# K's transposition on VectorE in 32x32 blocks instead of on TensorE, with K loaded in two halves, in a cached-attention and MLP decode kernel

## The chip, the cores and the metric

One Trainium2 chip, one core, float32 throughout. The metric is the device time of one execution in microseconds.

## The reference

A decode step of one transformer block (8 sequences, one token each) with adaptive layer norm. What is computed:

```python
mod = (silu(c) @ w_mod).reshape(8, 6, 1, 512)      # sa, ca, ga, sb, cb, gb
h = layernorm(x) * (1 + ca) + sa
x = x + ga * attention(h)
h = layernorm(x) * (1 + cb) + sb
x = x + gb * mlp(h)

def attention(x):                  # 32 query heads, 8 key heads, Dh = 128
    W = 2048                       # of 8192 cached keys, the last 2048 are used
    q = (x @ wq)                   # 512 -> 32*128
    k = repeat(k_cache[:, :, -W:], 4); v = repeat(v_cache[:, :, -W:], 4)
    p = softmax(q k^T * Dh**-0.5)
    return (p v) @ wo              # 32*128 -> 512

def mlp(x):                        # F = 1792
    r = max(x @ w1 + b1, 0)
    return (r * r) @ w2 + b2
```

The 8 sequences times 8 key heads give 64 pairs, each with a K and a V of 2048 x 128 numbers (1 MB each).

## The kernel before

**Loads.** All large loads are issued by the sync engine (SP) from one list, in a fixed order, into two "big" buffers (128 partitions x 32 KB: one K tile, which is four sequences of one key head, 4 MB) and five "small" ones (16 KB: one V tile, which is two sequences of one key head, 2 MB, or a piece of w_mod, wq or wo). `loads` (line 143) begins K0, w_mod in four pieces, wq in four pieces, K1, V0, K2, V1, K3, V2, V3, K4, and goes on with a K and two V in turn; biases, the last rows of wo, w1 and w2 end it. `pump` issues as long as the next load of the list has a free buffer. `done(key)` gives a buffer back and calls `pump`; SP then waits until the last reader of that buffer has finished, and every later load stands behind it.

In a K tile, partition 4p + u holds 64 successive keys of sequence u. `k` below is that tile as 64 columns (keys) of 128 numbers.

**The loop** (line 502) runs over the 32 halves of the 16 K tiles plus a lag of `PV_LAG` = 5 steps for V, and is written out by hand: nothing reorders it (`manual_schedule`). Each engine works through its own instructions in this order.

- `transposes(q, g, e)` (lines 223 to 238): eight transpositions of 128x128 by TensorE against the identity into PSUM (`kt_ps`), in two groups of four; ScalarE copies the first group out to `kT`, VectorE the second. Two calls (e = 0, 1) fill one of three `kT` buffers (four sequences of 512 columns). Eight calls make one K tile; the last gives the buffer back.
- `scores(q, g)` (346 to 364): four matmuls, one for each sequence u of the tile, with 32 columns of `qwin` stationary and the 512 columns `kT[:, u]` moving, into quarter u of the PSUM tile `s_ps`, which gathers all scores of one key head (two K tiles). `qwin` is a zero-padded window over q, so that each of the eight calls lands in rows of its own.
- `window(hk)` (343): one VectorE copy from `qall` into `qwin`.
- `soft_a` to `soft_d` (366 to 439): the softmax of one key head: copy out, row maximum, maximum over the rows of a pair (two small matmuls), exponential with its sum, a copy that doubles the columns, eight transpositions by TensorE, and two VectorE multiplications with the mask `mine` into `pT`.
- `weighted(n, h)` (441): P times V, four matmuls a call; after the second call of a V tile VectorE folds the result into `o_sb` with four instructions (464 and 466).
- `gather`, `project_o`: every fourth step, transposition of the head's output and its product with wo.

**The start.** While w_mod arrives, three quarters of K0 are transposed (`EARLY`, line 263, lets the loop skip them; the last quarter comes in the loop's step 0), between the matmuls on w_mod. After the last piece of wq, `turn_q(0)` (328) copies the first half of q out, turns it by four TensorE transpositions and copies it to `qall` (line 334); `turn_q(1)` does the second half in step 1. Then the scores begin.

**The end.** After the last V: output projection, residual, second layer norm, MLP; `spin` puts idle matmuls between.

Of the kernel before, what the change touches and what calls it, by code (L numbers as in the profile page):

```python
# [8 lines left out]
F32 = mybir.dt.float32  # L9
# [11 lines left out]
def tile_adaln_cached_attention_mlp(  # L21
# [15 lines left out]
    P = 128  # L37
# [18 lines left out]
    ktp = ctx.enter_context(tc.tile_pool(name="ktp", bufs=3))  # L56
    ps_kt = ctx.enter_context(tc.tile_pool(name="ps_kt", bufs=2, space=bass.MemoryType.PSUM))
# [32 lines left out]
    def load(key):  # L90
# [7 lines left out]
        if kind in "KV":  # L98
# [6 lines left out]
            v = v[:, SK - W :, :].rearrange("u (p j) d -> p u (j d)", p=P // v.shape[0])  # L105
# [79 lines left out]
    qall = consts.tile([P, HKV, B, REP], F32, name="qall")  # L185
    qwin = [consts.tile([P, B, 60], F32, name=f"qwin{i}") for i in range(2)]
    for t in qwin:
        nc.gpsimd.memset(t, 0.0)

# [8 lines left out]
    u4 = consts.tile([P, 4], F32, name="u4")  # L198
    nc.vector.tensor_reduce(u4, ident.rearrange("p (u x) -> p u x", u=4), axis=AX.X, op=ALU.add)
    for c in range(2):  # L200
        nc.vector.tensor_scalar(bq[:, 4 * c : 4 * c + 4], u4, uq[:, c : c + 1], None, op0=ALU.mult)
# [11 lines left out]

    mine = consts.tile([P, 2, REP], F32, name="mine")
    odd = ident.rearrange("p (r u) -> p u r", u=2)
    for u in range(2):
        nc.vector.tensor_reduce(mine[:, u, 0:1], odd[:, u, :], axis=AX.X, op=ALU.add)
        for t in range(1, REP):
            nc.vector.tensor_copy(mine[:, u, t : t + 1], mine[:, u, 0:1])

    KTS = {}

    def transposes(q, g, e):

        k = slot(("K", q), DH)
        if e == 0:
            KTS[q, g] = ktp.tile([P, 4, 16, 32], F32, name="kT")
        t = KTS[q, g]
        for a in range(2):
            p = ps_kt.tile([P, 4, P], F32, name="kt_ps")  # L230
            for i in range(4):
                nc.tensor.transpose(p[:, i, :], k[:, 32 * e + 16 * a + 4 * g + i, :], ident)  # L232
            i = 8 * e + 4 * a
            (nc.vector.tensor_copy if a else nc.scalar.copy)(  # L234
                t[:, :, i : i + 4, :], p.rearrange("p i (r u) -> p u i r", u=4)
            )
        if g == 3 and e == 1:
            done(("K", q))
# [24 lines left out]
    EARLY = [(0, g) for g in range(4)]  # L263
# [400 lines left out]
```

## Time and profile before

| | |
|---|---|
| median of 3 runs | 396.94 us (396.89 to 397.75) |
| the profiled execution | 397.39 us, of which the span from first to last instruction is 395.6 |
| TensorE busy | 330.5 us (84%) |
| VectorE busy | 178.2 us (45%) |
| ScalarE busy | 97.5 us (25%) |
| q1, the queue with all loads | 164.71 MB, 97.9% of 16 engines' span |
| read from HBM | 164.77 MB |
| mean granted clock of TensorE | 0.974 |

Busy time of an engine is the time in which it ran an instruction; idle time of an engine that is not the bottleneck costs nothing. In rows of groups the columns are line, engine, operation, output and inputs, shapes and count, then busy microseconds and the mean nanoseconds of one, then the idle time ahead of them and what ended it. In rows of stretches: from and to, length, busy time (count) of TensorE's matmuls, of its weight loads, of VectorE, ScalarE and GpSimd, the granted clock, the mean busy share of the 16 transfer engines, and GB/s. In rows of time: start, length, engine, line, operation. "PEld" is a weight load, "SPq" the queue of the engine that issues the loads.

### The profile page before, as it was taken

The numbers are of one execution on the slowest core, as the hardware profiler recorded it, in microseconds if no ns is written. First come the engines' busy times: TensorE is split into PE (matmuls) and PEld (weight loads), VectorE is DVE, ScalarE is ACT, GpSimd is POOL, SyncE is SP. The second block draws the span as 40 slices with busy tenths as digits, with TensorE's granted clock in tenths as the row PEclk, the third lists the DMA queues.
The fourth block names the chain that finished last, engine by engine and source line by source line (L and its number), as shares of the span: only waits on it lengthen the run. The fifth ranks groups of instructions, "written<-read, shape, count | busy, mean of one in ns | idle before, by whom it ended". The sixth has DMA issues, their size and how long they took to land.

```text
span 395.6 us, 5981 instructions
## 1 busy us (share of the span) xinstructions
PE 330.5 (84%) x2550; PEld 162.4 (41%) x2550; DVE 178.2 (45%) x416; ACT 97.5 (25%) x169; POOL 2.4 (1%) x12
## 2 busy tenths in 40 slices
PE   0683489979998697999889988998859998997696
PEld 0440035554454353444444544444534454432133
DVE  6121023454456353655464556454524455455531
ACT  2220022342232122322332222222211241222010
POOL 2000000000000000000000000000000000000000
PEclk9996889999999998999999999999999999999999
DMA  8999999999999999999999999999999999999993
GB/s 335 410 430 427 441 418 442 417 419 446 404 435 442 414 432 422 441 417 451 403 449 409 444 416 434 434 419 421 437 419 447 417 437 413 431 431 421 422 424 136
DMA packets 10363, 165.22 MB, mean 418 GB/s; under 512 B 1112, under 2 KB 1376, under 8 KB 1632
## 3 DMA queue, kind: packets, MB, share of 16 engines
q1 hardware_dynamic: 10192, 164.71, 97.9%
q8 instruction: 20, 0.33, 0.3%
q10 hardware_dynamic: 144, 0.13, 0.1%
q14 instruction: 7, 0.06, 0.0%
HBM read 164.77 MB, written 0.07 MB: 417 GB/s over the span
## 4 chain that ended last, share of the span: by engine, by line
DMA 46%; PE 42%; DVE 7%; ACT 4%; issue 1%; ACTq 0%; DVEq 0%
DMA big<-in_A_k_cache_dram 31%; PE kt_ps L232 20%; PE s_ps L358 9%; PE o_ps L450 7%; DMA small<-in_A_wq_dram 6%; DMA big<-in_B_w_dram 5%; DMA small<-in_A_v_cache_dram 4%; ACT pr L402 2%; DVE o_sb L466 2%; DVE kT L234 2%; PE m_ps L294 1%; ACT kT L234 1%; DVE pT L429 1%; PE m_ps L319 1%; DVE pr L410 1%
## 5 line engine op out<-in xcount | busy, mean ns | idle before, releaser
L232 PE MATMUL kt_ps<-ident,big 128*128 128x128 f32 x1024 | 145.5, 285 | 22.6 <-DMA big<-in_A_k_cache_dram 18.3
L232 PEld LDWEIGHTS kt_ps<-ident,big 128*128 128x128 f32 x1024 | 112.8, 144 | 111.9 <-ACT kT L234 68.1
L234 DVE COPY kT<-kt_ps 128x512 f32<-128x512 f32 x128 | 88.2, 689 | 121.5 <-PE kt_ps L232 121.5
L234 ACT COPY kT<-kt_ps 128x512 f32<-128x512 f32 x128 | 75.0, 586 | 209.4 <-PE kt_ps L232 208.6
L358 PE MATMUL s_ps<-kT,qwin 128*32 128x512 f32 x512 | 69.2, 614 | 0.8 <-DVE qwin L344 0.8
L450 PE MATMUL o_ps<-small,pT 128*32 128x512 f32 x512 | 67.1, 602 | 1.9 <-DMA small<-in_A_v_cache_dram 1.9
L466 DVE SCALAR_TENSOR_TENSOR o_sb<-o_ps,diag,o_sb 128x128 f32<-128x128 f32 x96 | 33.7, 351 | 3.4
L319 PE MATMUL m_ps<-small,h1T 128*32 128x512 f32 x64 | 11.5, 857 | 11.5 <-DMA small<-in_A_wq_dram 11.5
L450 PEld LDWEIGHTS o_ps<-small,pT 128*32 128x32 f32 x512 | 11.7, 108 | 22.7 <-issue 22.7
L464 DVE TENSOR_SCALAR o_sb<-o_ps,diag 128x128 f32<-128x128 f32 x32 | 11.2, 350 | 16.3 <-PE o_ps L450 15.6
L358 PEld LDWEIGHTS s_ps<-kT,qwin 128*32 128x32 f32 x512 | 10.3, 109 | 12.8 <-issue 11.1
L402 ACT ACTIVATE pr<-ss,nm 128x512 f32<-128x512 f32 x8 | 9.9, 1244 | 11.8 <-DVE nm L399 11.7
L334 DVE COPY qall<-m_ps 128x128 f32<-128x128 f32 x2 | 0.8, 390 | 23.0 <-PE m_ps L333 23.0
L435 PE MATMUL m_ps<-zs,tsel 128*128 128x8 f32 x16 | 3.1, 266 | 8.7 <-DVE pT L429 8.7
L319 PEld LDWEIGHTS m_ps<-small,h1T 128*32 128x32 f32 x64 | 2.1, 134 | 19.8 <-DMA small<-in_A_wq_dram 10.6
L429 DVE TENSOR_TENSOR pT<-m_ps,mine 128x512 f32<-128x512 f32 x16 | 10.2, 680 | 0.0
L474 PE MATMUL m_ps<-o_sb,pick 128*128 128x512 f32 x16 | 8.4, 606 | 1.8 <-DVE o_sb L466 1.6
L426 PEld LDWEIGHTS m_ps<-ident,pr 128*128 128x128 f32 x64 | 6.9, 141 | 7.0 <-issue 7.0
L426 PE MATMUL m_ps<-ident,pr 128*128 128x128 f32 x64 | 8.7, 278 | 1.1 <-DVE zs L412 1.1
L370 DVE TENSOR_REDUCE mx<-ss 128x1 f32<-128x512 f32 x8 | 5.5, 688 | 8.6 <-ACT ss L368 8.6
L410 DVE COPY pr<-pr 128x512 f32<-128x512 f32 x8 | 3.4, 430 | 12.3 <-ACT pr L402 12.3
L294 PE MATMUL m_ps<-small,cT 128*32 128x512 f32 (+1 forms) x64 | 6.6, 531 | 1.3 <-DMA small<-in_w_mod_dram 1.3
(123 smaller groups left out, 105.4 us busy)
## 6 DMA issues: line engine op xcount, KB each, us to landing
big<-in_A_k_cache_dram SPq DMA_DIRECT2D x16, 4096.0 KB, 21.9
small<-in_A_v_cache_dram SPq DMA_DIRECT2D x32, 2048.0 KB, 23.2
small<-in_A_wq_dram SPq DMA_DIRECT2D x4, 2048.0 KB, 21.8
small<-in_w_mod_dram SPq DMA_DIRECT2D x4, 1536.0 KB, 17.4
small<-in_A_wo_dram SPq DMA_DIRECT2D x3, 2048.0 KB, 19.9
big<-in_A_wo_dram SPq DMA_DIRECT2D x2, 1024.0 KB, 17.8
big<-in_B_w_dram SPq DMA_DIRECT2D x1, 2048.0 KB, 23.4
big<-in_B_w_dram SPq DMA_DIRECT2D x1, 1792.0 KB, 22.0
```

Of the source, the lines that this page charges most:

```text
L232: nc.tensor.transpose(p[:, i, :], k[:, 32 * e + 16 * a + 4 * g + i, :], ident)
L234: (nc.vector.tensor_copy if a else nc.scalar.copy)(t[:, :, i : i + 4, :], p.rearrange("p i (r u) -> p u i r", u=4))
L294: nc.tensor.matmul(pm[32 * q : 32 * q + 32, : (m1 - m0) * P].rearrange("p (m n) -> p m n", n=P), cT[:, kc, :], wv[:, m0:m1, q, :], start=( ...
L319: nc.tensor.matmul(pqs[r][32 * g : 32 * g + 32, :], hT[:, kc, :], w[:, 4 * r + g, :], start=(kc == 0), stop=(kc == NQ - 1),)
L358: nc.tensor.matmul(s_ps[0][32 * u : 32 * u + 32, :], qwin[hk % 2][:, 4 * c + u, o : o + 32], kT[:, u].rearrange("p i r -> p (i r)"), start ...
L402: nc.scalar.activation(pr.rearrange("p i (r e) u -> p e i r u", e=2)[:, :, :, :, 0], SS_.pop(hk).rearrange("p (e i r) -> p e i r", e=2, i= ...
L426: nc.tensor.transpose(pp[:, i * P : (i + 1) * P], pr[:, 4 * a + i].rearrange("p r u -> p (r u)"), ident)
L429: nc.vector.tensor_mul(PT_[hk][:, a].rearrange("p x i r -> p i x r"), pp.rearrange("p (i x r) -> p i x r", i=4, r=2 * REP), mine.rearrange ...
L450: nc.tensor.matmul(o[32 * g : 32 * g + 32].rearrange("p j d -> p (j d)"), PT_[hk][:, h, 4 * c + g].rearrange("p i r -> p (i r)"), v[:, j : ...
L464: nc.vector.tensor_scalar(d, o[:, 0, :], diag[:, 0:1], None, op0=ALU.mult)
L466: nc.vector.scalar_tensor_tensor(d, o[:, j, :], diag[:, j : j + 1], d, op0=ALU.mult, op1=ALU.add)
L474: nc.tensor.matmul(pp, pick.rearrange("p t u -> p (t u)"), o.rearrange("p c d -> p (c d)"), start=True, stop=True)
```

## The change

K's transposition goes to VectorE, whose transposition turns each 32x32 block of its operand in place. `transposes(q, j, e)` is now one VectorE instruction: 32 keys of each partition times the 32 numbers from 32j on, 1024 columns, written to `kT` in order. Eight calls still make a tile, but what lies on `kT`'s partitions is now 32 of the 128 numbers, for each of four groups of 32 partitions. So q is laid out in blocks: `turn_q` copies q with four instructions of 32 partitions each to `qbd`, and `window` multiplies it by `sel` on TensorE and copies the product with eight instructions (four each of ScalarE and VectorE) to `qst`. `scores` keeps four matmuls of 512 columns a call, but reads from `kT` pairs of columns, two out of every eight. For that the keys are spread otherwise over the partitions: each K is loaded by two DMAs, x = 0 and 1, into every second partition.

The rows of the scores then stand in another order. `soft_b` has one more matmul (128x512, with the permutation `perm`), the exponential reads its result from PSUM; the masked doubling is one instruction each of VectorE and ScalarE, and `soft_d` turns P with one VectorE transposition of 128x1024 instead of eight of TensorE and two multiplications. `kT` has two buffers instead of three, of the same size; the PSUM pool `ps_kt` is gone. `EARLY` holds half of K0, and the other half comes in the loop's step 1.

On SP each K is now two issues. Before, from the last piece of wq on (`big` a K buffer, `small` a V buffer):

```order
L113 DMA small_95<-in_A_wq_dram 128x4096
L108 DMA big_92<-in_A_k_cache_dram 128x1x8192
L108 DMA small_96<-in_A_v_cache_dram 128x1x4096
L108 DMA big_91<-in_A_k_cache_dram 128x1x8192
L108 DMA small_97<-in_A_v_cache_dram 128x1x4096
L108 DMA big_92<-in_A_k_cache_dram 128x1x8192
```

And now, at the same place:

```order
L117 DMA small_92<-in_A_wq_dram 128x4096
L107 DMA big_89<-in_A_k_cache_dram 64x1x8192 x2
L112 DMA small_93<-in_A_v_cache_dram 128x1x4096
L107 DMA big_88<-in_A_k_cache_dram 64x1x8192 x2
L112 DMA small_94<-in_A_v_cache_dram 128x1x4096
L107 DMA big_89<-in_A_k_cache_dram 64x1x8192 x2
```

The list is the same, each K stands in it twice with 64 partitions.

On VectorE, from the two halves of q (L334, `qall`) to the second K tile, before (L234 are the copies of K's transpositions out of PSUM, L344 the window):

```order
L310 TENSOR_SCALAR mul<-m_ps,lo 128x128
L334 COPY qall<-m_ps 128x4x32
L344 COPY qwin_115<-qall 128x8x4
L234 COPY kT<-kt_ps 128x4x128 x2
L334 COPY qall<-m_ps 128x4x32
L234 COPY kT<-kt_ps 128x4x128 x3
L344 COPY qwin_116<-qall 128x8x4
L234 COPY kT<-kt_ps 128x4x128 x6
L370 TENSOR_REDUCE mx<-ss 128x1
```

And now (L330 are the copies of q, L348 those of the window, L230 K's transpositions; big_88 holds K0, big_89 K1):

```order
L304 TENSOR_SCALAR mul<-m_ps,lo 128x128
L330 COPY qbd<-m_ps 32x4x4x8 x4
L348 COPY qst_113<-q_ps 32x16x4 x4
L330 COPY qbd<-m_ps 32x4x4x8 x4
L230 STREAM_TRANSPOSE kT<-big_88 128x1024 x4
L230 STREAM_TRANSPOSE kT<-big_89 128x1024 x3
L348 COPY qst_114<-q_ps 32x16x4 x4
L230 STREAM_TRANSPOSE kT<-big_89 128x1024 x5
L230 STREAM_TRANSPOSE kT<-big_88 128x1024
L375 TENSOR_REDUCE mx<-ss 128x1
```

K0's second half (big_88 x4) now stands behind twelve small copies, those of q's second half among them; before, two copies stand between q's first half and K0's last one.

On TensorE at the same place, before (L319 the product with wq, L333 q's transposition, L358 the scores, L232 K's transpositions):

```order
L319 MATMUL m_ps<-small_95,h1T 32x512 x8
L333 MATMUL m_ps<-ident,qs 128x128 x4
L358 MATMUL s_ps<-kT,qwin_115 32x512 x4
L232 MATMUL kt_ps<-ident,big_91 128x128 x16
L333 MATMUL m_ps<-ident,qs 128x128 x4
L358 MATMUL s_ps<-kT,qwin_115 32x512 x8
```

And now (L343 is the window's matmul):

```order
L313 MATMUL m_ps<-small_92,h1T 32x512 x8
L327 MATMUL m_ps<-ident,qs 128x128 x4
L343 MATMUL q_ps<-qbd,sel 128x128
L363 MATMUL s_ps<-kT,qst_113 32x512 x4
L327 MATMUL m_ps<-ident,qs 128x128 x4
L363 MATMUL s_ps<-kT,qst_113 32x512 x12
```

K's sixteen transpositions are gone, and the window's matmul stands ahead of the first scores.

```diff
-    ktp = ctx.enter_context(tc.tile_pool(name="ktp", bufs=3))
-    ps_kt = ctx.enter_context(tc.tile_pool(name="ps_kt", bufs=2, space=bass.MemoryType.PSUM))
+    ktp = ctx.enter_context(tc.tile_pool(name="ktp", bufs=2))
...
-            v = v[:, SK - W :, :].rearrange("u (p j) d -> p u (j d)", p=P // v.shape[0])
+            if kind == "K":
+                v = v[:, SK - W :, :].rearrange("u (h l j) d -> l h u (j d)", h=16, l=2)
+                for x in range(2):
+                    nc.sync.dma_start(t[x::2], v[x])
+                return
+            v = v[:, SK - W :, :].rearrange("u (p j) d -> p u (j d)", p=P // 2)
...
-    def transposes(q, g, e):
+    def transposes(q, j, e):
         k = slot(("K", q), DH)
         if e == 0:
-            KTS[q, g] = ktp.tile([P, 4, 16, 32], F32, name="kT")
-        t = KTS[q, g]
-        for a in range(2):
-            p = ps_kt.tile([P, 4, P], F32, name="kt_ps")
-            for i in range(4):
-                nc.tensor.transpose(p[:, i, :], k[:, 32 * e + 16 * a + 4 * g + i, :], ident)
-            i = 8 * e + 4 * a
-            (nc.vector.tensor_copy if a else nc.scalar.copy)(
-                t[:, :, i : i + 4, :], p.rearrange("p i (r u) -> p u i r", u=4)
-            )
-        if g == 3 and e == 1:
+            KTS[q, j] = ktp.tile([P, 64, 32], F32, name="kT")
+        rows = slice(32 * e, 32 * e + 32)
+        nc.vector.transpose(KTS[q, j][:, rows], k[:, rows, 32 * j : 32 * j + 32])
+        if j == 3 and e == 1:
             done(("K", q))
...
-    EARLY = [(0, g) for g in range(4)]
+    EARLY = [(0, 0), (0, 1)]
...
-        if kc < 3:
+        if kc < 2:
             transposes(0, kc, 0)
             transposes(0, kc, 1)
...
-        nc.vector.tensor_copy(
-            qall[:, 4 * r : 4 * r + 4].rearrange("p g b t -> p t g b"),
-            pT_.rearrange("p (t g b) -> p t g b", t=REP, g=4)[:, :, :, :B],
-        )
+        for j in range(4):
+            b = slice(32 * j, 32 * j + 32)
+            nc.vector.tensor_copy(
+                qbd[b, 4 * r : 4 * r + 4, j].rearrange("p g (b t) -> p t g b", t=REP),
+                pT_[b].rearrange("p (t g b) -> p t g b", t=REP, g=4)[:, :, :, :B],
+            )
...
     def window(hk):
-        nc.vector.tensor_copy(qwin[hk % 2][:, :, 28:32], qall[:, hk])
+        pq = ps_1.tile([P, 512], F32, name="q_ps")
+        nc.tensor.matmul(pq[:, :P], sel, qbd[:, hk].rearrange("p j x -> p (j x)"), start=True, stop=True)
+        pv = pq[:, :P].rearrange("p (j c u t) -> p c u j t", j=4, c=2, u=4)
+        for i in range(4):
+            b = slice(32 * i, 32 * i + 32)
+            for c in range(2):
+                (nc.vector.tensor_copy if c else nc.scalar.copy)(
+                    qst[hk % 2][b, 4 * c : 4 * c + 4, :, i, c], pv[b, c]
+                )
...
-        o = 28 - 4 * (2 * g + c)
-        kT = KTS.pop((q, g))
+        kT = KTS.pop((q, j)).rearrange("q r (h u l) -> q (r h) u l", u=4, l=2)
         for u in range(4):
             nc.tensor.matmul(
-                s_ps[0][32 * u : 32 * u + 32, :],
-                qwin[hk % 2][:, 4 * c + u, o : o + 32],
-                kT[:, u].rearrange("p i r -> p (i r)"),
-                start=(c == 0 and g == 0),
-                stop=(c == 1 and g == 3),
+                s_ps[0][32 * u : 32 * u + 32, :].rearrange("q (x l) -> q x l", l=2),
+                qst[hk % 2][:, 4 * c + u, j].rearrange("p i c t -> p (i c t)"),
+                kT[:, :, u],
+                start=(c == 0 and j == 0),
+                stop=(c == 1 and j == 3),
             )
...
     def soft_b(hk):
+        sp = ps_1.tile([P, 512], F32, name="p_ps")
+        nc.tensor.matmul(sp, perm, SS_.pop(hk), start=True, stop=True)
+        SS_[hk] = sp
...
-        nc.vector.tensor_copy(pr[:, :, :, 1], pr[:, :, :, 0])
+        X_[hk] = work.tile([P, 32, 8, 2, 2], F32, name="pr2", bufs=1)
+        for c in range(2):
+            o, i = X_[hk][:, :, :, :, c], pr.rearrange("p e j x -> p j x e")
+            if c:
+                nc.scalar.mul(o, i, uq[:, c : c + 1])
+            else:
+                nc.vector.tensor_scalar(o, i, uq[:, c : c + 1], None, op0=ALU.mult)
...
     def soft_d(hk):
-        pr = P_.pop(hk)
-        PT_[hk] = work.tile([P, 2, 4 * C, 4, 2 * REP], F32, name="pT", bufs=1)
-        for a in range(2):
-            pp = ps_m.tile([P, 512], F32, name="m_ps", tag="m_ps")
-            for i in range(4):
-                nc.tensor.transpose(
-                    pp[:, i * P : (i + 1) * P], pr[:, 4 * a + i].rearrange("p r u -> p (r u)"), ident
-                )
-            nc.vector.tensor_mul(
...
+        PT_[hk] = work.tile([P, 4, 32, 2 * REP], F32, name="pT", bufs=1)
+        nc.vector.transpose(
+            PT_[hk].rearrange("p u j r -> p j u r"),
+            X_.pop(hk).rearrange("p j (u r) e c -> p j u (r e c)", u=4),
+        )
...
-        if s == 0:
-            transposes(0, 3, 0)
-            transposes(0, 3, 1)
```

More of the change, by code (lines that the diff above doesn't have):

```diff
@@ L182, in tile_adaln_cached_attention_mlp @@
     s_ps = [None]
-    qall = consts.tile([P, HKV, B, REP], F32, name="qall")
-    qwin = [consts.tile([P, B, 60], F32, name=f"qwin{i}") for i in range(2)]
-    for t in qwin:
+    qbd = consts.tile([P, HKV, 4, B * REP], F32, name="qbd")
+    qst = [consts.tile([P, B, 4, 4, 2, REP], F32, name=f"qst{i}") for i in range(2)]
+    for t in [qbd, *qst]:
         nc.gpsimd.memset(t, 0.0)
```

51 lines of the change are left out of this document (16 added, 35 removed).

## The prediction

> **What bounds the kernel now.** I read the page first: the engines' busy shares, the transfer rate by slice, the DMA queues, the chain that ended last.
>
> ```profile
> span 395.6 us, 5981 instructions
> PE 330.5 (84%) x2550; PEld 162.4 (41%) x2550; DVE 178.2 (45%) x416; ACT 97.5 (25%) x169; POOL 2.4 (1%) x12
> q1 hardware_dynamic: 10192, 164.71, 97.9%
> q8 instruction: 20, 0.33, 0.3%
> DMA 46%; PE 42%; DVE 7%; ACT 4%; issue 1%; ACTq 0%; DVEq 0%
> ```
>
> TensorE is busy 84% and owns 42% of the chain, which invites the thought that taking the transpositions of K from it must pay. But the queue that carries K, V and the weights keeps the 16 transfer engines busy for 97.9% of the span. So the second view is busy time by stretch, for its last two columns (DMA share, GB/s):
>
> ```profile
> 0.00:17.00 17.00, 4.69 (x20) 4.00 (x20) 7.95 (x41) 4.80 (x8) 2.43 (x12) 1.00 0.89 366
> 17.00:60.00 43.00, 28.01 (x204) 10.28 (x206) 7.34 (x15) 5.12 (x10) 0.00 (x0) 0.84 1.01 428
> 140.00:220.00 80.00, 73.21 (x558) 36.81 (x555) 40.55 (x87) 22.07 (x38) 0.00 (x0) 0.98 1.01 430
> 300.00:380.00 80.00, 70.15 (x536) 31.09 (x528) 42.96 (x105) 18.64 (x33) 0.00 (x0) 1.00 1.01 427
> 386.00:388.00 2.00, 2.00 (x6) 0.72 (x4) 0.66 (x3) 0.00 (x0) 0.00 (x0) 1.00 0.75 305
> 388.00:390.00 2.00, 1.89 (x61) 1.65 (x64) 0.00 (x0) 0.00 (x0) 0.00 (x0) 1.00 0.54 215
> 390.00:392.00 2.00, 1.61 (x54) 1.10 (x44) 0.00 (x0) 0.00 (x0) 0.00 (x0) 1.00 0.18 61
> ```
>
> From 17 us to the end the transfers stand at 427 to 430 GB/s with a share of 1.0. The program moves 164.7 MB; at 430 GB/s that is 383 us, and what lies around it (2 us before the first byte, the ragged end from 386 us on, 4 us from the last byte to the stored result) makes the span. So nothing that TensorE saves in the middle can shorten the run, as long as the queue has work. Three things can move the end: a standstill of the queue, a change of its rate, and how unevenly the 16 transfer engines finish (shares 0.75, 0.54, 0.18 in the last rows).
>
> Third, what the queue waits for, and its issues near the start:
>
> ```profile
> SPq L108 <- PE kt_ps L232: 250.9, 30, 27.3
> 0.73 12.61 DMA big<-in_A_k_cache_dram
> 27.60 0.55 SPq L108 DMA_DIRECT2D big<-in_A_k_cache_dram  x1
> 30.04 0.54 SPq L108 DMA_DIRECT2D small<-in_A_v_cache_dram  x1
> 57.88 0.53 SPq L108 DMA_DIRECT2D big<-in_A_k_cache_dram  x1
> big<-in_A_k_cache_dram SPq DMA_DIRECT2D x16, 4096.0 KB, 21.9
> small<-in_A_v_cache_dram SPq DMA_DIRECT2D x32, 2048.0 KB, 23.2
> small<-in_A_wq_dram SPq DMA_DIRECT2D x4, 2048.0 KB, 21.8
> small<-in_w_mod_dram SPq DMA_DIRECT2D x4, 1536.0 KB, 17.4
> ```
>
> SP stands 250.9 us behind TensorE, for a K buffer to be read out (the longest wait, 27.3 us, ends at 57.88). These waits cost nothing while earlier loads are still on their way. Where is that margin smallest? Up to 30.04 SP has issued K0, four pieces of w_mod, four of wq, K1 and V0: 4.19 + 6.29 + 8.39 + 4.19 + 2.10 = 25.2 MB. By the rates above 6.2 MB have moved at 17 us and 18.4 more at 60 us, so these loads run dry near 61.4 us. K2 is issued at 57.88. K0, alone on its way, took 12.61 us for what takes 9.8 at 428 GB/s; of the 2.8 us that are not transfer I put half ahead of the first byte. So K2's data begins at 59.3, and the margin is 2.1 us. Later it is wide: the median K lands 21.9 us after its issue, 12 of which it stands behind others.
>
> **The change part by part.** Durations, from the groups by line and form:
>
> ```profile
> L232 PE MATMUL kt_ps<-ident,big 128*128 128x128 f32 x1024 | 145.5, 285 | 22.6 <-DMA big<-in_A_k_cache_dram 18.3 <-ACT kT L234 3.4
> L234 DVE COPY kT<-kt_ps 128x512 f32<-128x512 f32 x128 | 88.2, 689 | 121.5 <-PE kt_ps L232 121.5
> L234 ACT COPY kT<-kt_ps 128x512 f32<-128x512 f32 x128 | 75.0, 586 | 209.4 <-PE kt_ps L232 208.6 <-DVE kT L234 0.8
> L478 DVE STREAM_TRANSPOSE tr<-m_ps 128x512 f32<-128x512 f32 x8 | 5.7, 717 | 3.3 <-PE m_ps L474 3.3
> L243 DVE STREAM_TRANSPOSE rc<-m_ps 128x448 f32<-128x448 f32 x1 | 0.7, 650 | 1.3 <-PE m_ps L598 1.3
> L426 PE MATMUL m_ps<-ident,pr 128*128 128x128 f32 x64 | 8.7, 278 | 1.1 <-DVE zs L412 1.1
> L334 DVE COPY qall<-m_ps 128x128 f32<-128x128 f32 x2 | 0.8, 390 | 23.0 <-PE m_ps L333 23.0
> L399 DVE COPY nm<-m_ps 128x1 f32<-128x1 f32 x8 | 1.3, 157 | 4.1 <-PE m_ps L395 4.1
> L271 PE MATMUL m_ps<-xsum,sel 128*128 128x1 f32 x2 | 0.6, 363 | 8.4 <-DVE xsum L269 8.4
> L464 DVE TENSOR_SCALAR o_sb<-o_ps,diag 128x128 f32<-128x128 f32 x32 | 11.2, 350 | 16.3 <-PE o_ps L450 15.6
> L429 DVE TENSOR_TENSOR pT<-m_ps,mine 128x512 f32<-128x512 f32 x16 | 10.2, 680 | 0.0
> ```
>
> *K's transpositions.* 145.5 us leave TensorE, 75.0 ScalarE, 88.2 VectorE. VectorE gets 128 transpositions of 128x1024. No row has that size: 64 columns more (448 to 512) cost 67 ns, so 717 + 512 x 67/64 = 1.25 us; twice the 512 row is the upper bound (1.43), 1024 columns at the copy's rate without its fixed part the lower (about 1.05). I take 1.25: 160 us. A K tile then costs VectorE 8 x 1.25 = 10 us. With two V tiles (8 evictions of 0.35, 2.8 us), half a head's softmax, window copies and gather (about 4 us), that is 17 us, against 19.5 us in which the queue brings a K and two V (8.4 MB at 430). VectorE ends near 265 us of busy time. The cover is this 2.5 us. The next K is asked for about 12 us after the last one landed; now TensorE, busy 73 of 80 us, takes nearly the whole 19.5: the margin in the middle grows. The wait for K's landing moves from TensorE to VectorE; behind it there stand the evictions of o and the softmax, and for these P·V and the V buffers. They come late by no more than VectorE idles, and the 12 us that loads stand behind others cover that.
>
> *Scores, softmax, P·V.* Scores keep their 256 matmuls; that they read two columns and skip six is off the path even at twice their time, TensorE being down to about 190 us. The softmax loses 64 transpositions (8.7 us) and gains eight permutation matmuls, a second pass on VectorE and ScalarE and eight transpositions of 128x1024 (10 us): all between a K and the next, hidden by the same margin. If TensorE's clock falls in its new pauses, it has room for that too.
>
> *K in two loads.* 16 more issues of 0.55 us on SP, hidden: the queue holds 10 us of work when they come. Rows stay 32 KB. I cost the rate at nothing; the first rival is that this is wrong. The nearest rows, 427 to 430 GB/s, are for loads into all 128 partitions. [...]
>
> *The start.* Before: last piece of wq, q turned, window, scores, the last transpositions of K0, K2's issue:
>
> ```profile
> 49.52 3.45 PE L319 MATMUL m_ps<-small,h1T 128*32 128x512 f32 x16 [2.38 <-DMA small<-in_A_wq_dram]
> 52.91 0.66 PE L333 MATMUL m_ps<-ident,qs 128*128 128x128 f32 x4
> 53.60 0.38 DVE L334 COPY qall<-m_ps 128x128 f32<-128x128 f32 x1 [22.38 <-PE m_ps L333]
> 54.32 1.06 PE L358 MATMUL s_ps<-kT,qwin 128*32 128x512 f32 x8 [0.76 <-DVE qwin L344]
> 56.70 1.15 PE L232 MATMUL kt_ps<-ident,big 128*128 128x128 f32 x8 [0.29 <-ACT kT L234]
> 87.70 1.28 DVE L429 TENSOR_TENSOR pT<-m_ps,mine 128x512 f32<-128x512 f32 x2
> ```
>
> Now only half of K0 is turned early (two buffers of kT instead of three, each freed by its scores), and on VectorE the copies of both halves of q stand ahead of the other half. From 53.6: four copies of q (32 partitions, but as many columns as the 390 ns row) 1.56; the window's matmul and its weights 0.5 (363 ns row); four copies of 64 columns between 157 and 390, 0.27 each, 1.1; scores 1.06; q's second half on TensorE 0.66; its four copies 1.56; four transpositions 5.0. That is 65.1. VectorE starts an instruction some 0.08 us before the last one's end (two of L429's 0.68 us stand in 1.28): 12 of them, so 64.1. K2's data begins at 65.5: a standstill of 4.1 us after 61.4, for behind K2 on SP stand V1, K3 and every later load. Bounds: with 157 ns copies and 1.05 us transpositions 61.5 (a standstill of 1.5), with 390 ns and 1.43 us and no overlap 66.3 (6.3).
>
> *How unevenly it ends.* The standstill is worth less than its length, since the last transfer engine sets the end. [...] TensorE's 5100 instructions lose 2 x (1024 + 64) and gain 64: 2988, so 12 loads instead of 20. [...]
>
> The sum: + 4.1 - 1.0 - 1.6 = + 1.5 us. The profiled execution took 397.39 us (span 395.6 and 1.8 around it), 0.45 above the median of 396.94. So 398.9 by its own time, and 398.4 as a median.
>
> **The rivals.**
>
> *K's loads run slower.* If two transfer engines meet on the same part of SBUF when only every other partition is written, K's 67.1 MB take longer than their 156 us, and as the queue is the bound, each per cent costs 1.6 us; at half rate all 156 us, about 553 us. It decides from 1% on. [...] For it: no load of this trace has that form. [...] No row bears it out.
>
> *No standstill: faster.* If VectorE's small copies take 0.16 and the transpositions 1.05, and q comes a little earlier because K0 no longer interleaves on TensorE, K2 is issued by 61 and the standstill is under 1 us. With 1.6 saved at the end: 396.9 + 0.6 - 1.6 = 395.9. It decides if K2 is issued before 61.0.
>
> *About 2 us of standstill: no change.* K2 near 62.5, spread and loads give it back: 397.
>
> *VectorE becomes the bound.* At 1.25 us its 17 of 19.5 us leave room. From 1.6 us a transposition the room is gone; at 2.0 a K takes 23 us, 16 x 23 + 75 = 443. Against it: two rows of 512 and 448 columns at 1.4 ns a column.
>
> **How the numbers follow.** A standstill of 3 to 6 us, slower by 0.2 to 1%: 0.42. About 2 us: 0.25. None, faster: 0.13. K's loads clearly slower: 0.17. VectorE the bound: 0.03. I forecast 398.4. The range goes from 395.2 (a little below the faster case) to 406 (the upper bound of the standstill, 401, and up to 3% on K's loads) and leaves out the last two cases, 0.2; the likeliest case alone has 397.7 to 401. 0.2% of the time, 0.8 us, is about what a measurement here can tell from no change. Faster 0.13, same 0.25, slower 0.62.
>
> **What would show it.** Right: TensorE near 190 us busy, VectorE near 265, still 427 to 430 GB/s and a share of 1.0 from 70 us on, a stretch between 61 and 66 us with a share near 0, K2's first half issued near 64, about 12 instruction loads, transpositions of 1.25 us. Wrong: stretches with K in them below 420 GB/s, SP waiting on VectorE with the queue empty in the middle, or K2 issued before 61.

## The result, and the profile after

The changed kernel took 637.89, 640.76, 648.60 and 662.71 us in four runs (median 644.68). The last two count as slow runs, so the first two, 639.3 us on average, are compared with the kernel before, 397.12 us beside it: 1.6095 times as long, 95% interval 1.6025 to 1.6165. I had forecast 398.4 and a range of 395.2 to 406.

The page of the changed kernel: span, engines, rate by slice, queues, the chain that ended last.

```profile
span 636.1 us, 3803 instructions
PE 261.4 (41%) x1494; PEld 63.7 (10%) x1494; DVE 245.4 (39%) x430; ACT 33.4 (5%) x81; POOL 4.2 (1%) x13
GB/s 206 319 430 340 230 259 261 212 339 210 398 208 308 210 303 217 260 234 228 251 225 236 214 246 215 270 182 274 321 206 263 204 269 199 280 333 193 400 400 27
q1 hardware_dynamic: 10448, 164.71, 92.7%
q8 instruction: 12, 0.20, 0.1%
DMA 38%; another core or an unknown queue 25%; DVE 20%; PE 14%; ACT 1%; issue 1%; SPq 1%; DVEq 0%; ACTq 0%
```

No engine has become the bound: TensorE is busy 41%, VectorE 39%. The queue still is (92.7%), with the same 164.71 MB. But the rate is no longer a steady 430: it swings between 182 and 430. The same by stretches (the last two columns are DMA share and GB/s):

```profile
0.00:10.00 10.00, 0.59 (x2) 0.50 (x2) 7.66 (x30) 1.59 (x2) 4.23 (x13) 1.00 1.01 220
10.00:20.00 10.00, 0.58 (x2) 0.50 (x2) 0.54 (x3) 2.04 (x4) 0.00 (x0) 1.00 1.00 213
30.00:40.00 10.00, 7.59 (x44) 1.78 (x48) 0.01 (x1) 0.00 (x0) 0.00 (x0) 1.00 1.02 433
160.00:170.00 10.00, 1.74 (x8) 0.23 (x8) 4.75 (x8) 0.00 (x0) 0.00 (x0) 0.50 1.00 412
180.00:190.00 10.00, 6.51 (x36) 1.35 (x36) 3.98 (x6) 0.20 (x1) 0.00 (x0) 0.84 0.99 211
320.00:400.00 80.00, 31.69 (x157) 7.73 (x158) 33.73 (x54) 3.02 (x8) 0.00 (x0) 0.63 0.91 225
```

From 0 to 20 us only K0 is on its way: the transfer engines are busy all the time (share 1.0) and move 213 to 220 GB/s, half of what they move at 30 to 40 us, when w_mod and wq come. So a share of 1.0 says that the engines have work, not that they are fast; the two columns are read together. This is the rival "K's loads run slower" at half rate, which I gave 0.17. Its 553 us fall 86 short, though. The waits, the landing times and the groups (mean ns of one in the second number after the bar):

```profile
SPq L107 <- DVE kT L230: 274.1, 14, 36.6
77.97 1.18 SPq L107 DMA_DIRECT2D big<-in_A_k_cache_dram  x2
big<-in_A_k_cache_dram SPq DMA_DIRECT2D x32, 2048.0 KB, 47.3
small<-in_A_v_cache_dram SPq DMA_DIRECT2D x32, 2048.0 KB, 53.5
L230 DVE STREAM_TRANSPOSE kT<-big 128x1024 f32<-128x1024 f32 x128 | 151.8, 1219 | 255.0 <-DMA big<-in_A_k_cache_dram 254.9
L363 PE MATMUL s_ps<-kT,qst 128*32 128x512 f32 x512 | 97.6, 841 | 277.3 <-DVE kT L230 273.9
```

VectorE waits 254.9 us for K to land, TensorE 273.9 us for VectorE, and SP 274.1 us for VectorE before it may load the next K: each stands behind the transfers. Two questions: why half rate, and what are the other 86 us?

### The profile page after: what moved, and what is told of

It reads as the page before. It is cut to its first block, busy times and chain, and to the rows that moved or that the text cites. A ratio compares the mean times of both kernels' runs of the same rounds, so it can differ in the third digit from the quotient of the medians.

```text
span 636.1 us, 3803 instructions
## 1 busy us (share of the span) xinstructions
PE 261.4 (41%) x1494; PEld 63.7 (10%) x1494; DVE 245.4 (39%) x430; ACT 33.4 (5%) x81; POOL 4.2 (1%) x13
## 3 DMA queue, kind: packets, MB, share of 16 engines
q1 hardware_dynamic: 10448, 164.71, 92.7%
## 4 chain that ended last, share of the span: by engine, by line
DMA 38%; another core or an unknown queue 25%; DVE 20%; PE 14%; ACT 1%; issue 1%; SPq 1%; DVEq 0%; ACTq 0%
DMA big<-in_A_k_cache_dram 26%; DVE kT L230 12%; DMA small<-in_w_mod_dram 5%; PE s_ps L363 4%; DMA small<-in_A_wq_dram 4%; PE o_ps L446 3%; DMA small<-in_A_v_cache_dram 3%; DVE o_sb L462 2%; PE p_ps L380 2%; DVE pT L426 1%; PE q_ps L543 1%; ACT pr L404 1%; DVE o_sb L460 1%; DVE mx L375 1%
## 5 line engine op out<-in xcount | busy, mean ns | idle before, releaser
L230 DVE STREAM_TRANSPOSE kT<-big 128x1024 f32<-128x1024 f32 x128 | 151.8, 1219 | 255.0 <-DMA big<-in_A_k_cache_dram 254.9
L363 PE MATMUL s_ps<-kT,qst 128*32 128x512 f32 x512 | 97.6, 841 | 277.3 <-DVE kT L230 273.9
L446 PE MATMUL o_ps<-small,pT 128*32 128x512 f32 x512 | 87.0, 759 | 45.4 <-DMA small<-in_A_v_cache_dram 45.3
L363 PEld LDWEIGHTS s_ps<-kT,qst 128*32 128x32 f32 x512 | 14.4, 130 | 326.3 <-DVE kT L230 168.4
L348 ACT COPY qst<-q_ps 32x64 f32<-32x64 f32 x32 | 6.5, 203 | 193.9 <-DVE qst L348 110.6
L380 PE MATMUL p_ps<-ss,perm 128*128 128x512 f32 x16 | 15.7, 1079 | 0.0
L330 DVE COPY qbd<-m_ps 32x128 f32<-32x128 f32 x8 | 3.0, 369 | 26.1 <-PE m_ps L327 26.1
L426 DVE STREAM_TRANSPOSE pT<-pr 128x1024 f32<-128x1024 f32 x8 | 9.8, 1230 | 0.0
L348 DVE COPY qst<-q_ps 32x64 f32<-32x64 f32 x32 | 6.8, 213 | 7.4 <-ACT qst L348 7.4
L486 PE MATMUL wo_ps<-small,oT 128*32 128x512 f32 x48 | 7.5, 695 | 0.0
L412 ACT ACTIVATE pr<-pr,uq 128x512 f32<-128x512 f32 x8 | 6.8, 848 | 0.3
```

The lines of the kernel that those rows point to most:

```text
L230: nc.vector.transpose(KTS[q, j][:, rows], k[:, rows, 32 * j : 32 * j + 32])
L348: (nc.vector.tensor_copy if c else nc.scalar.copy)(qst[hk % 2][b, 4 * c : 4 * c + 4, :, i, c], pv[b, c])
L363: nc.tensor.matmul(s_ps[0][32 * u : 32 * u + 32, :].rearrange("q (x l) -> q x l", l=2), qst[hk % 2][:, 4 * c + u, j].rearrange("p i c t -> ...
L380: nc.tensor.matmul(sp, perm, SS_.pop(hk), start=True, stop=True)
L426: nc.vector.transpose(PT_[hk].rearrange("p u j r -> p j u r"), X_.pop(hk).rearrange("p j (u r) e c -> p j u (r e c)", u=4),)
L446: nc.tensor.matmul(o[32 * g : 32 * g + 32].rearrange("p j d -> p (j d)"), PT_[hk][:, c, j : j + 4].rearrange("p i r -> p (i r)"), v[:, j : ...
```

## The experiments

A *block* below is one entry of the slowest dimension of what a load reads: the K of before is read as 32 blocks (p) of 4 rows (u), the changed kernel's halves as 16 blocks (h) of 4 rows.

**e1: the loads alone undone.**

```diff
-                v = ....rearrange("u (h l j) d -> l h u (j d)", h=16, l=2)
-                for x in range(2):
-                    nc.sync.dma_start(t[x::2], v[x])
+                v = ....rearrange("u (p j) d -> p u (j d)", p=32)
+                nc.sync.dma_start(t, v)
...
-        kT = KTS.pop((q, j)).rearrange("q r (h u l) -> q (r h) u l", u=4, l=2)
+        kT = KTS.pop((q, j)).rearrange("q r (h u) -> q (r h) u", u=4)
...
```

> The changed kernel, but each K comes in one load into all 128 partitions, as before the change, and the scores read single columns instead of pairs. Everything else (transpositions on VectorE, softmax, order) stays. Theory 1, the form of K's loads is the whole loss: the transfers go back to 427 to 430 GB/s and what is left is what I forecast for the rest of the change, 398.4 us (397.7 to 401), K2 issued near 64 us. Rival, VectorE or the scores hold the K buffers too long, and the slow loads only follow from that: above 600 us still, with rates far below 427.

402.49 us, 1.0123 times the kernel before (1.0105 to 1.0142). The stretches, SP's K2, the scores:

```profile
60.00:70.00 10.00, 7.61 (x37) 1.06 (x36) 9.52 (x11) 0.20 (x1) 0.00 (x0) 1.00 0.34 112
140.00:220.00 80.00, 57.37 (x300) 11.73 (x304) 58.58 (x96) 6.06 (x16) 0.00 (x0) 0.88 1.01 430
66.63 0.54 SPq L106 DMA_DIRECT2D big<-in_A_k_cache_dram  x1
L362 PE MATMUL s_ps<-kT,qst 128*32 128x512 f32 x512 | 127.4, 1074 | 85.3 <-DVE kT L229 78.9
```

The form of the loads is worth 237 of the 242 us; the rest of the change, VectorE's transpositions and all, costs 5.3. Those five go with the standstill at the start that I forecast, which lasts somewhat longer: the share is 0.34 between 60 and 70 us, and 430 GB/s are back from 140 us on.

**e2: in the kernel before, K in two loads of alternate partitions, no row skipped.**

```diff
+            if kind == "K":
+                for x in range(2):
+                    nc.sync.dma_start(t[x::2], v[:, x::2])
+                return
```

> The kernel before, with one edit: each K comes in two loads, one of the even and one of the odd partitions; each reads the whole window of two batches of the four, so no 32 KB of a window is skipped, and every row goes where it went. Theory 1a, writing every other partition is what halves the rate: K's 67.1 MB take 312 instead of 156 us, so 553 us at least, up to 645 if it loses as much as the changed kernel. Theory 1b, reading every other 32 KB is what halves it: 397 us, no change. Rival, VectorE: 397 us.

397.18 us, ratio 0.9993 (0.9962 to 1.0023), with 428 GB/s from 140 to 220 us:

```profile
140.00:220.00 80.00, 75.02 (x584) 37.65 (x583) 42.10 (x91) 22.44 (x39) 0.00 (x0) 1.00 1.00 428
```

Theory 1a falls: neither two loads instead of one nor alternate partitions cost anything that these runs can tell from no change. What differs from the changed kernel is only which rows a half reads: here 32 blocks of 2 rows, there 16 of 4.

**e3: forms of loads by themselves.**

> Loads alone, no attention: eleven stages one after the other, each waits until the one before has landed, the first ten 8.39 MB each, the last 16.8 MB. At 428 GB/s a stage's transfers take 19.6 us, at half rate 39.2. Stages: (1) whole K; (2) alternate partitions with every other 32 KB, as in the changed kernel; (3) alternate partitions, no 32 KB skipped; (4) 128 partitions from every other 32 KB; (5) two contiguous halves of 64 partitions; (6) 128 partitions, halves of the columns; (7) every fourth partition, four loads; (8) contiguous quarters; (9) as 2, odd partitions issued by ScalarE; (10) V alone; (11) the changed kernel's K and V in turn. Theory 1a (every other partition on the writing side): 20, 39, 39, 20, 20, 20, 39 or more, 20, 20 to 39, 20. Theory 1b (every other 32 KB on the reading side): 20, 39, 20, 39, 20, 20, 20, 20, 20 to 39, 20. Theory 1c (any load of fewer than 128 partitions): 20, 39, 39, 20, 39, 20, 39 to 78, 39 to 78, 20 to 39, 20. Stage 11: 58.8 us if only K is slow (39.2 for two K, 19.6 for four V), more if V is slowed by its neighbour.

Some loads of the last stage ran ahead, beside other stages, so its stage times can't be read; e7 repeats it. Its rates still showed the changed kernel's form (210 GB/s from 30 to 50 us) and "128 partitions from every other 32 KB" (201 from 130 to 146) both at half, which made me believe in the reading side, every other 32 KB. I passed over two stages that skip no row and are at half all the same. Two contiguous halves ran at 208 GB/s (175 to 190 us, share 0.99). Contiguous quarters, whose loads have 8 blocks, ran at 213 to 217, but with a share of 0.49 to 0.50: there half of the time of the 16 engines was without work. At 210 and a share near 1.0, all engines had work, and moved half of what they move at 430.

**e4: the changed kernel's loads, nothing computed.**

> The changed kernel's loads in their order and form into its 2 and 5 buffers, with nothing computed: a buffer is free as soon as it has landed and one small VectorE instruction has read two of its columns. Tells the 82 us that the changed kernel lies above half rate (636 of span against 552 to 555) apart. If the waits for buffers cost them: about 550 us. If V and the weights are slowed beside K: near 630 us. If VectorE is the cause of it all: about 390 us.

A span of 558.4 us (one run): near the 552 to 555 of half rate alone, and 78 us less than the changed kernel. VectorE's small readings of K:

```profile
q1 hardware_dynamic: 10448, 164.71, 98.9%
251.80 0.16 DVE L180 TENSOR_TENSOR acc<-big 128x1 f32<-128x1 f32 x1 [19.11 <-DMA big<-in_A_k_cache_dram]
281.69 0.16 DVE L180 TENSOR_TENSOR acc<-big 128x1 f32<-128x1 f32 x1 [18.94 <-DMA big<-in_A_k_cache_dram]
```

A K lands every 29.9 us: 19 for K, 11 for the two V.

**e5: e1 with V1 and V2 ahead of K2.**

```diff
-loads = [..., ("K", 1), ("V", 0), ("K", 2)]
+loads = [..., ("K", 1), ("V", 0), ("V", 1), ("V", 2), ("K", 2)]
...
```

> As e1 (whole loads of K, single columns), and V1 and V2 stand ahead of K2 in the list of loads. In e1 the transfers stood still from about 60 to 67 us, until K2 was issued at 66.63. Theory: that standstill is all that e1 loses against the kernel before; 4.2 MB of V move the moment at which the queue runs dry from 61 to 71 us, K2 is in time, and with 12 instruction loads instead of 20 the time is 395 to 396.5 us, 402.5 less 6 to 7. Rival, what e1 loses comes also from scores that read single columns or from VectorE: 398 to 402 us, with transfers below 427 GB/s somewhere else.

402.65 us (ratio 1.0127, 1.0104 to 1.0150), nothing gained. The standstill has moved, as the rival in effect had it: 60 to 70 us run full, and now 95 to 100 us have

```profile
95.00:100.00 5.00, 2.86 (x14) 0.81 (x18) 5.00 (x8) 0.38 (x1) 0.00 (x0) 0.66 0.18 75
100.92 0.54 SPq L106 DMA_DIRECT2D big<-in_A_k_cache_dram  x1
```

K4 is the late one now: K2, behind two V, lands later, and VectorE is still behind with the work that it got when q came.

**e6: the changed kernel, other rows.**

```diff
-                v = ....rearrange("u (h l j) d -> l h u (j d)", h=16, l=2)
+                v = ....rearrange("u (p j) d -> p u (j d)", p=32)
                 for x in range(2):
-                    nc.sync.dma_start(t[x::2], v[x])
+                    nc.sync.dma_start(t[x::2], v[:, x::2])
```

> The changed kernel word for word, two loads of alternate partitions and scores by pairs of columns, but for the rows that the two loads read: each load takes the whole window of two batches instead of every other 32 KB of four (so half of K's rows stand at another row's place, and the attention is not the reference's). Theory A, which 32 KB are read sets the rate: 427 to 430 GB/s and 400 to 403 us, like e1. Rival, writing alternate partitions in VectorE's company, or reading pairs, costs something: above 410 us. If pairs of columns are worth something against e1's single ones, s_ps falls from 127 us towards 98, and the time stays.

402.78 us (ratio 1.0121, 1.0093 to 1.0149). Word for word the changed kernel but for the source of two loads, and 237 us are back:

```profile
140.00:220.00 80.00, 49.91 (x298) 11.57 (x298) 58.56 (x95) 6.06 (x16) 0.00 (x0) 0.83 1.01 429
```

The time is where theory A has it. But the edit also makes 32 blocks of 2 rows out of 16 of 4, so this run can't tell "which 32 KB" from "how many blocks". Its scores by pairs of columns take 764 ns against 1074 by single ones in e1: the pairs do what they are for, off the path.

**e7: the forms again, in order.**

> Loads alone, in the order written, eleven stages of 8.39 MB, each after the one before has landed (in e3 some loads of the last stage ran early, beside other stages). 19.6 us of transfer at 428 GB/s, 39.2 at half rate. Stages: (1) whole K; (2) as the changed kernel; (3), (4), (5) 16 windows of which every other 8, 16, 32 KB is read, 128 partitions; (6) two successive rows of 32 KB of each of 64 heads; (7) eight successive rows of each of 16 heads; (8) contiguous halves of the partitions, each from the whole window of two batches; (9) alternate partitions, each load one half (512 KB) of the window of four batches; (10) alternate partitions, each load the whole window of two batches; (11) V. Theory A, the address of a 32 KB block, odd or even, sets the half: 20, 39, 20, 20, 39, 20, 20, 20, 20, 20, 20. If smaller blocks count as well, 3 and 4 are 39. Theory B, a load whose slowest dimension of the source is 16 is slow (true of all the slow forms in e3): 20, 39, 39, 39, 39, 20, 39, 20, 39, 20, 20. If the half of the partitions counts on the writing side, 8 is 39.

Stages 2 (as the changed kernel), 8 (contiguous halves of the partitions), 9 (alternate partitions, each load a successive half of the window) and 10 (as in e6). In the rows of loads alone there are two engines, VectorE and GpSimd, between the length and the clock:

```profile
28.00:64.00 36.00, 1.27 (x8) 0.00 (x0) 1.00 1.01 215
283.00:316.00 33.00, 1.27 (x8) 0.00 (x0) 1.00 1.00 207
328.00:362.00 34.00, 1.27 (x8) 0.00 (x0) 1.00 0.99 208
373.00:388.00 15.00, 1.27 (x8) 0.00 (x0) 1.00 0.98 420
```

Theory A falls: stage 9 skips no 32 KB and runs at 208. Theory B names stage 9 rightly and stage 8 wrongly: 8 and 10 read in the same form, 32 blocks of two batches, and differ in the partitions alone (207 against 420 GB/s). So the writing side counts. Stages 3 to 7 step through whole heads, 4 MB apart, as only one more stage here does (e10's fourth, 375 GB/s); 3 to 5 and 7 ran at 211 to 228, 6 at 296, and nothing is concluded from them.

**e8: e4, with each K held for 14 transpositions.**

```diff
+        for _ in range(14 if key[0] == "K" else 0):
+            nc.vector.transpose(turned, t[:, :1024].rearrange("p (r x) -> p r x", x=32))
...
```

> As e4, loads alone (558 us of span), but VectorE holds each K for 14 transpositions of 128x1024, 17 us, before its buffer is free (in the changed kernel K's turning takes about that, from its landing to the next issue). If late release of K's buffers makes the 78 us between e4 and the changed kernel: 600 to 640 us. If not: 558 to 570, since the queue holds 30 to 40 us of work when a K lands.

A span of 637.7 us (one run): the changed kernel's 636.1 are reached with no attention in it.

```profile
q1 hardware_dynamic: 10448, 164.71, 95.2%
265.79 17.88 DVE L182 STREAM_TRANSPOSE turned<-big 128x1024 f32<-128x1024 f32 x14 [18.76 <-DMA big<-in_A_k_cache_dram]
309.61 17.88 DVE L182 STREAM_TRANSPOSE turned<-big 128x1024 f32<-128x1024 f32 x14 [19.49 <-DMA big<-in_A_k_cache_dram]
```

A K now comes every 39 to 44 us instead of every 29.9. Holding K for 18 us is enough to cost 79 us, and in the changed kernel a K is held about that long (landed at 322.0 and 360.9, next issues at 340.0 and 378.5). By their shares the transfer engines were busy 552 us in e4, 607 in e8 and 590 in the changed kernel: part of the loss is transfers that last longer, part engines without work. How the one leads to the other isn't shown. Nor does e8 hold K alone: VectorE works in order, so a V that lands during the hold is given back behind it (two of them at 246.7). At full rate VectorE's turning of K costs the queue nothing from 140 us on (e1, 430 GB/s).

**e9: the changed kernel, K in four loads of every fourth partition.**

```diff
-                for x in range(2):
-                    nc.sync.dma_start(t[x::2], v[x])
+                for x in range(4):
+                    nc.sync.dma_start(t[x::4], v[x % 2][:, x // 2 :: 2])
```

> The changed kernel with the same rows of K at the same places, but each K in four loads of every fourth partition instead of two of every second one (each load: every other 32 KB, two of the four batches; the slowest dimension of the source is still 16). [...] B: a load whose slowest source dimension is 16 runs at half rate; then this one does too, 630 to 660 us. [...]

622.61 us in the profiled run, four runs from 622.61 to 644.30, with 223 GB/s while K0 is alone on its way:

```profile
0.00:10.00 10.00, 0.59 (x2) 0.50 (x2) 7.66 (x30) 1.59 (x2) 4.23 (x13) 1.00 0.98 223
```

Theory C, that the order of an engine's rows sets the rate, had this run at full rate and falls (e10 puts it to the test once more). 16 blocks stay slow with two rows in each; the profiled run is a little under theory B's 630.

**e10: order of an engine's rows.**

> Loads alone, six stages of 8.39 MB, as in e7: (1) every fourth partition, source as in e9; (2) every eighth partition, eight loads in the order 0 to 7, one row for each engine and load, every other 32 KB; (3) the same eight loads in the order 0, 4, 1, 5, 2, 6, 3, 7; (4) four successive rows of each of 32 heads into 128 partitions; (5) as the changed kernel; (6) whole K. Theory C (the order of an engine's rows over blocks of four partitions): 20, 39, 20, 20, 39, 20 us; stages 2 and 3 are the same loads in another order. Theory B (16 in the slowest source dimension): 39, 39, 39, 20, 39, 20. Theory A (every other 32 KB of the source, which e7's stages 7 and 9 speak against): 39, 39, 39, 20, 39, 20.

Stages 1 to 3:

```profile
5.00:38.00 33.00, 1.27 (x8) 0.00 (x0) 1.00 1.00 222
46.00:80.00 34.00, 1.27 (x8) 0.00 (x0) 1.00 1.01 210
92.00:126.00 34.00, 1.27 (x8) 0.00 (x0) 1.00 1.03 229
```

They run at 222, 210 and 229 GB/s. The same eight loads in another order both run at about half, which is the second blow to theory C. Stages 5 and 6, the controls, 210 and 411.

**e11: e1, with VectorE relieved at the start.**

```diff
-    EARLY = [(0, 0), (0, 1)]
+    EARLY = [(0, 0), (0, 1), (0, 2)]
...
+            if (q, j) == (0, 2):
+                KTS[q, j] = work.tile([P, 64, 32], F32, name="kT2", tag="pr2", bufs=1)
...
-        if s == 1:
+        if s == 3:
             turn_q(1)
...
+    first = [("K", 1), ("V", 0), ("V", 1), ("V", 2), ("K", 2), ("K", 3), ("V", 3), ("V", 4), ("K", 4), ("wo", 0)]
...
```

> A try at a better kernel on e1's base: three quarters of K0 turned before q is there (the third kT buffer lies where the softmax's product lies later), the other half of q turned three steps later, and V1, V2, and V4 loaded ahead of K2 and K4. In e1 the transfers stand still from 61 to 68 us, in e5 from 95 to 101, both times because VectorE is behind with K0, K1 and K2 after q came at 53.5. Theory: five us less for VectorE after q and 5 to 10 us more transfers in the queue take most of that away, 396 to 399 us. Rival: the backlog only moves to a later K: 401 to 403.

398.29 us (ratio 1.0026, 1.0015 to 1.0037). Of the 5.3 us four are back; what is left stands between 100 and 105 us (share 0.75, 265 GB/s), before K4:

```profile
100.00:105.00 5.00, 4.71 (x34) 0.98 (x30) 4.16 (x7) 0.20 (x1) 0.00 (x0) 1.00 0.75 265
```

**e12: 16 blocks or 32.**

> Loads alone, six stages of 8.39 MB, to part theory A (every other 32 KB of the source) from theory B (16 blocks in the slowest dimension of the source, one for each transfer engine) for good; theory C fell with e9 and e10. Stages, all by rows of 32 KB but the fifth: (1) every other 32 KB, 32 blocks of each of four batches, 128 partitions; (2) every other 32 KB, 16 blocks of each of eight batches, 128 partitions; (3) every other 32 KB, 64 blocks of each of two batches; (4) two loads of alternate partitions and alternate 32 KB as in the changed kernel, but 32 blocks of each of two batches instead of 16 of four; (5) the changed kernel's own loads cut in two by columns, rows of 16 KB; (6) successive 32 KB, 16 blocks of each of eight batches. Theory B: 20, 39, 20, 20, 39, 39 us. Theory A: 39, 39, 39, 39, 39, 20. In between, some 25 to 30 us, would say that the number of blocks works by how the engines fall out of step, as with the 64 heads of e7 (28 us).

The six stages:

```profile
5.00:22.00 17.00, 1.27 (x8) 0.00 (x0) 1.00 1.00 432
28.00:66.00 38.00, 1.27 (x8) 0.00 (x0) 1.00 0.99 207
75.00:90.00 15.00, 1.27 (x8) 0.00 (x0) 1.00 1.02 441
98.00:115.00 17.00, 1.27 (x8) 0.00 (x0) 1.00 1.01 434
122.00:158.00 36.00, 1.91 (x12) 0.00 (x0) 1.00 1.00 219
165.00:202.00 37.00, 1.27 (x8) 0.00 (x0) 1.00 0.96 200
```

Every stage is where theory B has it. 32 or 64 blocks: full rate, though every other 32 KB is skipped. 16 blocks: half, skipped or successive, rows of 16 or 32 KB. Stage 4 is the changed kernel's own pair of loads but for 32 blocks of two batches in place of 16 of four: 434.

**e13: do the engines get in each other's way where they write, or where they read?**

> Loads alone, seven stages of 8.39 MB: 16 blocks of 32 KB in each load, into 16 partitions that lie 1 (stage 1), 2 (2), 4 (3) and 8 (4) apart, the source the same (every other 32 KB of a batch); then 32 successive blocks into 32 partitions 1 (5), 2 (6) and 4 (7) apart. Stages 4 and 7 repeat forms already seen, 39 and 20 us. [...] Theory E, they get in each other's way where they read, whichever partitions are written: stages 1 to 4 all 39, 5 to 7 all 20.

The seven stages:

```profile
5.00:68.00 63.00, 1.27 (x8) 0.00 (x0) 1.00 1.01 116
80.00:116.00 36.00, 1.27 (x8) 0.00 (x0) 1.00 0.99 206
127.00:160.00 33.00, 1.27 (x8) 0.00 (x0) 1.00 1.03 216
170.00:206.00 36.00, 1.27 (x8) 0.00 (x0) 1.00 0.99 204
215.00:250.00 35.00, 1.27 (x8) 0.00 (x0) 1.00 1.01 210
260.00:296.00 36.00, 1.27 (x8) 0.00 (x0) 1.00 0.99 204
305.00:322.00 17.00, 1.27 (x8) 0.00 (x0) 1.00 1.00 432
```

The first four stages read in the same form, and yet 16 neighbouring partitions are filled at 116 GB/s and partitions 2, 4 or 8 apart at 204 to 216. Stages 5 to 7 read in one form too: 32 partitions that lie 1 or 2 apart are filled at 210 and 204, 4 apart at 432. So with the same form of source, the places written set the rate. Theory E, the reading side, falls. What makes some places slow no view here shows.

**e14: e11 with V2 behind K2.**

```diff
-("V", 1), ("V", 2), ("K", 2), ("K", 3), ("V", 3), ...
+("V", 1), ("K", 2), ("V", 2), ("K", 3), ("V", 3), ...
```

> As e11, but V2 stands behind K2 instead of ahead of it. In e11 what is left of the standstill is at 100 to 105 us (265 GB/s), before K4, which waits for K2's turning; K2 landed at 83.4, behind V1 and V2. With V2 behind it K2 lands 5 us earlier and K4 is asked for near 96, before the queue runs dry at 101. Theory: no standstill left, and 12 instruction loads instead of 20: 396 to 396.8 us, under the kernel before by 0.1 to 0.3%. Rival, K3 or K5 come late in its place: 398 to 399.

396.32 us against 397.15, ratio 0.9975 (0.9965 to 0.9984): faster than the kernel before, by a quarter of a per cent.

```profile
60.07 0.54 SPq L106 DMA_DIRECT2D big<-in_A_k_cache_dram  x1
95.66 0.54 SPq L106 DMA_DIRECT2D big<-in_A_k_cache_dram  x1
100.00:105.00 5.00, 2.57 (x16) 0.30 (x12) 4.17 (x8) 0.61 (x3) 0.00 (x0) 1.00 1.03 442
```

K2 is asked for at 60.1, K4 at 95.7, and the stretch that stood in e11 runs at 442. With whole loads and no standstill, the span is 394.6 against 395.6. How much of the 1 us is the change's own isn't shown: e14 has another order of V and K too, and the kernel before was not run with that order.

## Why the prediction was wrong, point by point

- **K in two loads, the step that failed.** "I cost the rate at nothing." It was the dearest term of all: about +156 us by the rate (e4) and about +80 behind it (e8), where I had nothing. That K comes in two loads was indeed free (e2, 0.9993 times before), and so were alternate partitions (e2 and e6, 428 and 429 GB/s). In these runs a load's rate goes with two things: into how many blocks its source falls (16: 200 to 219 GB/s, 32 or 64: 432 to 441, e12; 16 stay slow in whatever order of loads, e9 and e10) and, with the same form of source, which partitions it writes (207 against 420 in e7, 116 to 216 and 204 to 432 in e13). K's loads in the changed kernel, 16 blocks into 64 alternate partitions, ran at 215 (e7, stage 2). How the two belong together isn't shown. My rival had the half rate; that only every other partition is written does not bring it about by itself (e2). I set it at 0.17 because "No row bears it out"; but no row spoke against it either, and a term of 156 us, with its 553 us written down beside it, deserved more than a rate taken from loads of another form.
- **Why the loads before escaped.** A K of before falls into 32 blocks and a V into 64, and loads of 32 and 64 blocks into all 128 partitions ran at 432 and 441 GB/s by themselves (e12, stages 1 and 3). That they fill all 128 partitions is not what spared them: 16 blocks into all 128 ran at 207 and 200 (stages 2 and 6). Which engine wrote which partition no trace here shows, and why 16 blocks are slow and 32 not stays open.
- **The price of the rival.** 553 us left out that a K at half rate fills the queue's margin: e4 gives 558 for the loads alone, e8 638 once each K is held 18 us. "The margin in the middle grows" was true at full rate only: there a K lands 24.0 us after its issue (e1, median) against 21.9 before, and the queue loses nothing.
- **TensorE's savings are worth nothing** because the queue is the bound: right. e1, e6 and e14 run at 427 to 430 GB/s from 140 us on, and all end within 1.3% of before.
- **VectorE's transpositions:** 1.25 us forecast, 1.22 measured; VectorE 265 us busy forecast, 245 measured. It never became the bound of the middle.
- **TensorE** ended at 261 us, not near 190: scores by pairs take 841 ns where the old ones took 614 in the profile of before, and P times V, of the same shape as before, takes 759 instead of 602, at a granted clock of 0.63 to 0.69 (stretches of 80 us from 80 to 560) where it was 0.98 to 1.00. Off the path in either case.
- **The start.** K2 at 64.1 forecast, 66.63 in e1 (77.97 in the changed kernel, where q comes 11 us later, behind K0 at half rate). The terms that were short: the eight copies of the window run one after another, VectorE and ScalarE in turn, 1.9 us instead of 1.1, and the first scores take 2.00 instead of 1.06. The standstill is 6.6 us (share 0.34 of ten), above my upper bound of 6.3.
- **How unevenly it ends.** 12 instruction loads as forecast (q8: 20 before, 12 in the changed kernel and in e1). The sum gives 1.0 and 1.6 us back, for the engines' unevenness at 60 us and at the end; no run shows either term, since no view here tells one transfer engine from another. In their place e1 shows that 6.6 us of standstill became 5.3 of span, so 1.3 came back, not 2.6. In e14, without a standstill, the span is 1.0 shorter than before; that the fewer instruction loads did that isn't shown.
- **The sum without the failed step** was 398.4 (397.7 to 401); e1 says 402.5, slower as forecast, by 5.3 us where I had 1.5.

## What to carry to other kernels

Where the queue is the bound, first ask of every changed load into how many blocks its slowest dimension falls and which partitions it writes; a load of 64 alternate partitions ran at 434 GB/s with 32 blocks (e12, stage 4) and at 215 with 16 (e7, stage 2), and the same form of source into 32 partitions at 210 when they lie side by side and at 432 when they lie 4 apart (e13). Read the DMA share and the GB/s side by side: in these runs a share of 1.0 at half the rate was engines that all had work and moved half as much (215 GB/s, e7), a share of 0.5 engines without work (217, e3). And a term without any row behind it is to be bounded by what its worst mechanism would cost, with a chance to match, before a few microseconds at the start are worked out to a tenth.

## What the runs showed of the hardware that I had not expected

- Loads whose slowest source dimension is 16 ran at 200 to 219 GB/s, those with 32 or 64 at 432 to 441 (e12), into 64 alternate partitions or all 128, rows of 32 KB (16 KB in the stage at 219). With heads 4 MB apart as the slowest dimension, 64 blocks ran at 296 (e7) and 32 at 375 (e10).
- Two loads that write a contiguous half of the partitions each ran at 207 GB/s even with 32 blocks, alternate halves with the same form of source at 420 (e7).
- 16 rows into 16 neighbouring partitions: 116 GB/s; 32 rows into 32 partitions 1 or 2 apart 204 to 210, 4 apart 432 (e13).
- Loads of 8 blocks kept the transfer engines busy half of the time: share 0.50, 217 GB/s (e3).
- Holding a buffer 18 us, shorter than the 20 us that one K takes at half rate, cost 79 us over 16 K (e4, e8, one run each), though by my estimate the queue held 30 to 40 us of work (a K landed 54.3 us after its issue in e4, median, about 19 of them its own transfer).
